# Three of seven pairs of chunk 0's gradient product moved into the opening part, and the steps that go with it

## The chip, the cores and the metric

The kernel runs on one core of a Trainium2 chip, as one launch. The metric is the device time of that launch in microseconds, lower is better. PE is the matrix engine (TensorE), ACT the scalar engine, DVE the vector engine, POOL the GpSimd engine; SP only issues DMAs. PE writes its products to PSUM banks, and ACT or DVE must copy ("evict") them to SBUF before a bank is used again.

## What is computed

A four-layer network and its gradients, with S = 2048 positions, D = 448 features, F = 1792 hidden features, in bfloat16. Cut to what matters:

```python
def A(q, k, v, shift_k, ssm_k, ssm_D):     # long convolution, done by FFT
    kv = short_conv(k, shift_k) * v
    y = irfft(rfft(kv, 2S) * rfft(ssm_k, 2S))[:S] + kv * ssm_D
    return q * y
def B(x, w1, w2):
    return silu(x @ w1) @ w2
x = A_q
x = x + A(layernorm(x), ...)
x = x + B(layernorm(x), w1, w2)
x = x + A(layernorm(x), ...)               # the same k, v: y is the same
x = x + B(layernorm(x), w1, w2)
# outputs: x, and the gradients of q, k, v, shift_k, ssm_k, ssm_D, w1, w2 for a given grad_out
```

## The kernel before

**Opening part** (`_ssm_prefix`). It computes y once. The spectrum of ssm_k is made first (A1K, Z, Ka in the lines); then kv goes through a two-stage FFT. Stage 1 ends at A1kv, which is turned by PE transposes in seven groups (`turn`, L367; a `ps_tr` tile and a copy each). Then a loop over 14 chunks of 1024 columns (`_fft_stage2` with `cons_prod`, L461) does, for each chunk: two matmuls into `ps_s`, an eviction, one DVE product `pab` with the spectrum and its half-swapped copy, and, two chunks later, 16 short matmuls into `ps_v` with an eviction. Evictions go to ACT or DVE by `_Bal.pick`, which adds up estimated loads. The half-swapped copy is made by 14 DMAs on POOL's queue (L440); after them come the stores of the spectrum (L445). All PSUM tiles here share four slots, tag "A". Last, eight `ps_y` tiles give Ysb, all evicted by ACT (L497). The layer norm of chunk 0's input (`ln0`, `_ln_steps`) is fed into this part by `next(ln0)`.

**Main part** (`Main.run`). Positions are worked in four chunks of 512. The blocks, named by the letters of the `weave` patterns, are:

- H: product with w1, seven pairs of hidden tiles; ACT computes silu (aT) and copies the raw value (dT), so a pair costs ACT two evictions. L is the layer, 0 or 1.
- O: product of aT with w2, added to X; eight half steps of 7 matmuls, two to each tile of 128 positions; its two PSUM banks are freed by the DVE addition L699.
- G: product of a gradient with w2 transposed, seven pairs, evicted by ACT to ghT, later multiplied by the slope of silu on DVE.
- N: product of ghT with w1 transposed, eight half steps, then the layer norm's gradient on DVE.
- T: PE transposes with an ACT copy to nT or gT, the input of H or G.

`_products` (L504) yields the seven pairs of H or G: pair 0 has 8 matmuls, pairs 1, 3, 5 have 10 (four of them on half the rows), pairs 2, 4, 6 have 6. PE's order is the program's order; the other engines are ordered by a scheduler from its own estimates. `slope` (L683) is the ACT pass that turns dT into slopes after each H block. `fwd0(c)` and `fwd0b(c)` compute, on DVE with a power on POOL, layer 0's normalised and gated input of chunk c and from it n01, which T transposes for the next H.

For chunk 0, grad_out is transposed at the end of the opening part into gT0, a piece of X (L484 to 488). Its G block runs as three pairs before the first H (L816) and four behind the first O (L828). Chunk 1's G follows: three pairs at L831, and four at c = 1 in the pattern `OGGOGGOTOT` (L858). The input of chunk 1's G is loaded by eight transposing DMAs on SP's queue (`load_gT`). Loads on SP in this part are, in order: x0c for chunk 1, w2sb, w1T, gb, then these.

Of the kernel before, what the change touches and what calls it, by code (L numbers as in the profile page):

```python
# [10 lines left out]
FP32 = mybir.dt.float32  # L11
# [249 lines left out]
def _ln_steps(k, pool, c, src, si, n_g, groups=((0, 4),), pin=False, eng=None, behind=None, store=()):  # L261
    nc = k.nc
    for lo, hi in groups:
        n = hi - lo
        st = pool.tile([P, 4, 6], FP32, name="ln_st", tag="ln_st", bufs=1)
        mv = pool.tile([P, 4, 2], FP32, name="ln_mv", tag="ln_mv", bufs=2)
        for tl in range(lo, hi):
            with ExitStack() as es:
                if behind:
                    es.enter_context(k.tc.issue_after(behind[tl].ins))  # L270
                i = nc.vector.bn_stats(out=st[:, tl, :], in_=src(tl))
            if pin:
# [6 lines left out]
        k.ln_pow = nc.gpsimd.tensor_tensor(out=r[:, lo:hi], in0=ve[:, 0:n], in1=k.mhalf[:, 0:n], op=ALU.pow)  # L279
        if eng is nc.scalar:  # L280
            nmr = pool.tile([P, 4], FP32, name="ln_nmr", tag="ln_nmr", bufs=1)
            nc.vector.scalar_tensor_tensor(out=nmr[:, lo:hi], in0=mv[:, lo:hi, 0], scalar=-1.0, in1=r[:, lo:hi], op0=ALU.mult, op1=ALU.mult)
        for tl in range(lo, hi):
            if eng is nc.scalar:
                nc.scalar.activation(n_g[:, tl, :], src(tl), ACT.Identity, bias=nmr[:, tl:tl + 1], scale=r[:, tl:tl + 1])
            else:
                k.ln_last = nc.vector.tensor_scalar(out=n_g[:, tl, :], in0=src(tl), scalar1=mv[:, tl, 0:1], scalar2=r[:, tl:tl + 1], op0=ALU.subtract, op1=ALU.mult)  # L287
# [10 lines left out]
def _ssm_prefix(k):  # L298
# [4 lines left out]
    with ExitStack() as es:  # L303
# [60 lines left out]
        bal.reset()  # L364
        A1Kf = A1K[:].rearrange("p a c n s -> p (a c n s)").rearrange("p (a b) -> p a b", b=P)

        def turn(src, dst, g):  # L367
            pt = psum.tile([P, 16, P], BF16, name="ps_tr", **a_)
            for i in range(16):
                nc.tensor.transpose(pt[:, i, :], src[:, 16 * g + i, :], k.ident[:])  # L370
            _copy(nc, bal.pick(2048, dve_ns=0.53), dst[:, 16 * g:16 * g + 16, :], pt[:])

        for jq in range(4):
            pt = psum.tile([DC, ND, 4, P], BF16, name="ps_kT", **a_)
# [50 lines left out]
        for h in range(2):  # L425
            for i, jq in enumerate((1, 2, 3, 0)):
                kvt = conv(h, jq)
                if prev:
                    stage1_kv(*prev)
                prev = (h, jq, kvt)  # L430
                if h == 0:
                    for g in (2 * i, 2 * i + 1):
                        if g < 7:
                            turn(A1Kf, Z, g)
                else:
                    _fft_stage2(k, Z, psum, cons_ka, range((0, 4, 8, 11)[i], (4, 8, 11, 14)[i]))
                    next(ln0, None)
        for _ in ln0:
            pass
        for i in range(7):  # L440
            _swap_halves_dma(k, KB, Ka, 2048 * i, 2048 * (i + 1), nc.gpsimd)
        stage1_kv(*prev)
# [4 lines left out]
        nc.sync.dma_start(out=k.w1sb[:, 0:3, :], in_=k.B_w1[0:384].rearrange("(c p) f -> p c f", p=P))  # L447
        nc.sync.dma_start(out=k.w1sb[64:128, 3, :], in_=k.B_w1[384:448, :])
        nc.sync.dma_start(out=k.w1sb[0:64, 3, 2 * P:], in_=k.B_w1[320:384, 2 * P:])
        nc.gpsimd.memset(k.w1sb[0:64, 3, 0:2 * P], 0.0)  # L450


# [2 lines left out]

        A1f = A1kv[:].rearrange("p a c n s -> p a (c n s)")
        for g in range(7):
            turn(A1f, Zkv, g)
        hold = []

        def cons_prod(ci, ps):  # L461
            sl = slice(ci * 1024, (ci + 1) * 1024)
            xs = Zf[:, sl]
            _copy(nc, bal.pick(1024), xs, ps[:])
            if ci % 2 == 1:
                st = nc.gpsimd.dma_start(out=k.SPEC_d["KV"][:, (ci - 1) * 1024:(ci + 1) * 1024], in_=Zf[:, (ci - 1) * 1024:(ci + 1) * 1024])
            if ci == 3:
                with tc.issue_after(st.ins):
                    nc.gpsimd.memset(k.w2T[0:64, 3, 0:2 * P], 0.0)
            pab = work.tile([P, 2, 1024], BF16, name="pab", tag="pab", bufs=3)  # L470
            nc.vector.tensor_tensor(out=pab[:], in0=xs.rearrange("p (a c) -> p a c", a=1).to_broadcast([P, 2, 1024]), in1=ZK[:, :, sl], op=ALU.mult)
# [8 lines left out]
        k.X = k.wk.tile([P, NT, D], BF16, name="X", tag="WX")  # L480
        k.gT0 = k.X[:].rearrange("p t d -> p (t d)")[:, 11 * D:11 * D + 2048].rearrange("p (b t) -> p b t", b=ND)
        for pa, pb, cj in hold:
            _fft_inv_stage2_chunk(k, pa, pb, False, B1, cj, psum, halves=cj == NCI - 1)
        pt = psum.tile([P, ND, 512], BF16, name="ps_t", tag="A", bufs=4)  # L484
        for b, (lo, hi) in enumerate(BLK):
            for tl in range(4):
                nc.tensor.transpose(pt[:, b, tl * P:(tl + 1) * P], k.gb0[:, tl, lo:hi], k.ident[:])
        nc.vector.tensor_copy(k.gT0, pt[:])

        B1v = B1.rearrange("p a (c n s) -> p a c n s", c=2, n=16)  # L490
        for i in range(8):
            py = psum.tile([P, 2, 512], FP32, name="ps_y", tag="A", bufs=4)
# [45 lines left out]
class Main:  # L538
# [165 lines left out]
    def G(self, gT, res, dT=None, dv=()):  # L704
        nc, k = self.nc, self.k
        half = lambda h: self.t([P, NF // 2, 512], f"ghT{h}", "T", 5)
        res[:] = [half(0)]
        gh = res
        for fp, ps in _products(nc, lambda: self.banks("ps_g"), self.w2T, gT):
# [74 lines left out]
    def run(self, es):  # L784
# [34 lines left out]
        aT, dT1 = r  # L819
# [17 lines left out]
        for c in range(4):  # L837
# [38 lines left out]
            if c < 3:  # L876
                r = []
                if c == 0:
                    weave("NTNTNHNNHHNNHHNHH", N=n, T=self.T(self.n0[1][1], nT), H=self.H(c + 1, 0, nT, r, (10, 11)))
# [23 lines left out]
            if c < 3:  # L903
                r = []
                nT = self.nT()
                weave("NNTNTNHNNHHNNHHHH", N=n, T=self.T(self.n1[1], nT), H=self.H(c + 1, 1, nT, r, (10, 11)))
            else:
                weave("NJNNJNNJNNJN", N=n, J=jg)
        jobs.pool = None
# [473 lines left out]
```

## Time and profile before

| what | value |
|---|---|
| time before, median of 3 runs | 716.89 us (713.9 to 718.23) |
| the profiled execution's own time | 716.31 us |
| its span in the trace | 714.5 us |
| PE busy | 689.3 us, 96% of the span |
| DVE busy / ACT busy | 486.2 us / 444.2 us |
| POOL busy | 123.3 us |

The sum of a prediction is made against the profiled execution: 716.31 us, of which 714.5 us is the span and 1.8 us lies around it. In a timeline, the first two columns are start and duration in us; the bracket at the end is the time the engine sat idle before that row, and what ended that idle time. Neighbouring instructions of one kind are merged into a row with a count, and a row's duration ends with its last instruction, so that back to back rows overlap a little.

### The profile page before, as it was taken

How to read it: one execution, taken by the hardware profiler on the slowest of the kernel's cores; microseconds unless marked ns; L12 is line 12 of the kernel's file. 1: busy time of each engine (PE TensorE's matmuls, PEld its weight loads, DVE VectorE, ACT ScalarE, POOL GpSimd, SP SyncE). 2: the span in 40 equal slices, each digit the busy share in tenths (PEclk: the TensorE clock that was granted, in tenths of full speed). 3: DMA queues.
4: the chain of work that ended last, by engine and by line, in shares of the span. 5: the costliest groups of instructions: out<-in, count | busy, mean ns of one | idle time of the engine just before them, and what ended most of it. 6: DMA issues, size and time to landing. Idle time of an engine off the chain costs nothing.

```text
span 714.5 us, 12786 instructions
## 1 busy us (share of the span) xinstructions
PE 689.3 (96%) x5008; PEld 380.9 (53%) x5008; DVE 486.2 (68%) x1106; ACT 444.2 (62%) x582; POOL 123.3 (17%) x208
## 2 busy tenths in 40 slices
PE   6997899999999999999999999999999999999998
PEld 4886654434444444444444444544566666656655
DVE  4788776758887747877279723934258769869790
ACT  3878877686777868778677685132755555545200
POOL 1034420111011100111001100001212223353130
PEclk9999899999999999999999999999999999999999
DMA  9949998659969999499975999089999897879962
GB/s 303 305 146 234 342 287 255 168 139 270 236 146 235 215 240 242 116 243 231 224 179 133 233 229 365 3 187 249 309 413 357 291 343 245 266 274 377 354 181 95
DMA packets 196237, 172.59 MB, mean 242 GB/s; under 512 B 143090, under 2 KB 174194, under 8 KB 195024
## 3 DMA queue, kind: packets, MB, share of 16 engines
q1 hardware_dynamic: 181280, 115.30, 61.3%
q0 software_dynamic: 13344, 52.54, 20.9%
q10 hardware_dynamic: 1552, 3.94, 1.5%
q8 instruction: 39, 0.64, 0.4%
q14 instruction: 22, 0.18, 0.1%
HBM read 73.25 MB, written 60.10 MB: 187 GB/s over the span
## 4 chain that ended last, share of the span: by engine, by line
PE 62%; issue 8%; DVE 5%; ACT 4%; DMA 3%; POOL 2%; POOLq 0%; DVEq 0%; ACTq 0%
PE ps_d L995 12%; PE ps_n L741 12%; PE ps_h L513 11%; PE ps_g L513 10%; PE ps_o L695 7%; PE ps_d L1030 3%; ACT dT L688 2%; DMA ksf<-KS_d 1%; PE ps_t L580 1%; PE ps_gK L1305 1%; PE ps_tr L1211 1%; POOL rstd L279 1%; PE ps_d L1065 1%; PE ps_s L206 1%; DVE n L287 1%
## 5 line engine op out<-in xcount | busy, mean ns | idle before, releaser
L995 PEld LDWEIGHTS <-dstat 128*128 128x128 bf16 x768 | 72.5, 98 | 61.1
L513 PE MATMUL ps_h<-nT,w1sb 128*128 128x512 bf16 (+1 forms) x448 | 97.4, 380 | 2.6 <-ACT dT L678 1.9
L741 PE MATMUL ps_n<-w1T,ghT 128*128 128x448 bf16 x448 | 92.5, 353 | 0.8 <-DVE ghT L866 0.8
L695 PE MATMUL ps_o<-w2sb,aT 128*128 128x448 bf16 x448 | 88.5, 352 | 0.0
L513 PE MATMUL ps_g<-nT,w2T 128*128 128x512 bf16 (+1 forms) x392 | 82.9, 380 | 0.1
L723 ACT CAST ghT<-ps_g 128x512 bf16<-128x512 f32 (+1 forms) x74 | 54.1, 760 | 41.5 <-PE ps_g L513 41.2
L673 ACT ACTIVATE aT<-ps_h 128x512 bf16<-128x512 f32 (+1 forms) x82 | 60.0, 759 | 29.2 <-PE ps_h L513 27.6
L513 PEld LDWEIGHTS <-w1sb 128*128 128x128 bf16 (+1 forms) x448 | 35.5, 97 | 59.7 <-issue 25.4
L741 PEld LDWEIGHTS <-ghT 128*128 128x128 bf16 x448 | 43.2, 98 | 42.3 <-DVE ghT L866 1.7
L695 PEld LDWEIGHTS <-aT 128*128 128x128 bf16 x448 | 43.5, 98 | 40.1
L513 PEld LDWEIGHTS <-w2T 128*128 128x128 bf16 (+1 forms) x448 | 35.4, 97 | 55.1 <-issue 20.8
L915 DVE SCALAR_TENSOR_TENSOR lb_v<-lb_u,n 128x448 bf16<-128x448 bf16 x48 | 30.0, 624 | 46.8 <-ACT lb_u L745 46.3
L279 POOL TENSOR_TENSOR rstd<-ln_ve,mhalf 128x2 f32<-128x2 f32 (+2 forms) x27 | 23.0, 851 | 198.8 <-DVE ln_ve L277 198.8
L688 ACT ACTIVATE dT<-dT 128x1024 bf16<-128x1024 bf16 (+1 forms) x64 | 55.0, 940 | 0.1
L995 PE MATMUL ps_d<-n1m,dstat 128*128 128x448 bf16 x224 | 48.6, 352 | 0.0
L995 PE MATMUL ps_d<-n3m,dstat 128*128 128x448 bf16 x224 | 48.6, 352 | 0.0
L678 ACT CAST dT<-ps_h 128x1024 bf16<-128x1024 f32 (+1 forms) x50 | 42.8, 872 | 0.0
L745 ACT ACTIVATE lb_u<-ps_n,rstd 128x448 bf16<-128x448 f32 x32 | 20.7, 647 | 34.5 <-PE ps_n L741 26.3
L995 PE MATMUL ps_d<-X,dstat 128*128 128x448 bf16 x160 | 34.2, 353 | 0.0
L995 PE MATMUL ps_d<-go,dstat 128*128 128x448 bf16 x160 | 33.7, 353 | 0.0
L581 ACT COPY nT<-ps_t 128x1024 bf16<-128x1024 bf16 x20 | 20.2, 1008 | 18.7 <-PE ps_t L580 18.7
L866 DVE TENSOR_TENSOR ghT<-dT,ghT 128x512 bf16<-128x512 bf16 (+2 forms) x24 | 18.1, 778 | 19.2 <-ACT ghT L723 17.0
(217 smaller groups left out, 1245.1 us busy)
## 6 DMA issues: line engine op xcount, KB each, us to landing
dstat<-g_d SPq DMA_DIRECT2D x28, 512.0 KB, 5.6
dstat<-a_d SPq DMA_DIRECT2D x23, 512.0 KB, 7.1
a_d<-turned SPq DMA_DIRECT2D x16, 512.0 KB, 4.1
g_d<-turned SPq DMA_DIRECT2D x16, 512.0 KB, 3.9
a_d<-turned SPq DMA_DIRECT2D x16, 384.0 KB, 3.3
g_d<-turned SPq DMA_DIRECT2D x16, 384.0 KB, 3.3
N_d<-n POOLq DMA_DIRECT2D x10, 448.0 KB, 4.6
spec_K<-ZK POOLq DMA_DIRECT2D x7, 512.0 KB, 7.7
```

Of the source, the lines that this page charges most:

```text
L279: k.ln_pow = nc.gpsimd.tensor_tensor(out=r[:, lo:hi], in0=ve[:, 0:n], in1=k.mhalf[:, 0:n], op=ALU.pow)
L513: nc.tensor.matmul(ps(u, u + 1)[:, 0, :], lhsT=wT[h, b, ft * P:(ft + 1) * P], rhs=rhs[h, b, :], start=start, stop=stop)
L673: self.last_silu = nc.scalar.activation(aT[hh][:, o:o + hi - lo, :], ps(lo, hi), ACT.Silu)
L678: nc.scalar.copy(self.dpart(dT, 2 * fp + lo, 2 * fp + hi), ps(lo, hi))
L688: self.nc.scalar.activation(d[:, o:o + n, :], d[:, o:o + n, :], ACT.Derivative_silu)
L695: nc.tensor.matmul(po[:, :D], lhsT=aT[ft // 7][:, ft % 7, tl * P:(tl + 1) * P], rhs=self.w2sb[:, ft, :], start=(ft == 0), stop=(ft == NF - 1))
L723: nc.scalar.copy(g, ps(lo, hi))
L741: nc.tensor.matmul(pn[:, :D], lhsT=gh[ft // 7][:, ft % 7, tl * P:(tl + 1) * P], rhs=self.w1T[:, ft, :], start=(ft == 0), stop=(ft == NF - 1))
L745: nc.scalar.activation(u0[:], pn[:, :D], ACT.Identity, scale=k.rstd[2 * L + 1][:, t:t + 1], accum_out=cp[:, tl, 0:1])
L915: nc.vector.scalar_tensor_tensor(out=v[:], in0=u0, scalar=-1.0 / D, in1=n_t, op0=ALU.mult, op1=ALU.mult, accum_out=cp[:, 1:2])
L995: self.nc.tensor.matmul(ps[:, :D], lhsT=st[:, t, :], rhs=mov[:, t, :], start=(first and t == 0), stop=(last and t == NT - 1))
L1030: nc.tensor.matmul(ps[ft][:, :D], lhsT=get(t), rhs=mov[:, t, :], start=ft not in seen, stop=(last[ft] == i and t == hi - 1))
```

## The change

Chunk 0's gradient is transposed in front of the 14-chunk loop instead of behind it. Three blocks of its product with w2 (pairs 0, 1 and 2) are issued in the opening part: behind chunk 6, behind chunk 10 and behind the loop. The other four pairs run in front of the first H. The first seven hidden tiles (gh0) live in X, in rows that chunk 2 and 3 fill later; so the G of chunk 0's layer 0 uses that place too. Chunk 1's whole G block follows the first O, and nothing of G is left at c = 1. With it go: the layer norm `ln0` starts earlier (its steps also run in the loop's first half), w1sb is loaded through POOL's queue behind the spectrum stores, a memset of w2T comes earlier, the seven turns are dealt out to ACT and DVE by hand, `fwd0b(1)` follows the six slope products, and two weave patterns are changed (the first of N of layer 1 with H of chunk 1, the second of N of layer 0 with H of layer 1). Of the three loads of w1sb the diff shows one.

```diff
 def _ln_steps(...)
         k.ln_pow = nc.gpsimd.tensor_tensor(out=r[:, lo:hi], ..., op=ALU.pow)
+        yield
 def _ssm_prefix(k):
-        def turn(src, dst, g):
+        def turn(src, dst, g, eng=None):
...
-            _copy(nc, bal.pick(2048, dve_ns=0.53), dst[:, 16 * g:16 * g + 16, :], pt[:])
+            _copy(nc, eng or bal.pick(2048, dve_ns=0.53), dst[:, 16 * g:16 * g + 16, :], pt[:])
...
                             turn(A1Kf, Z, g)
+                    next(ln0)
                 else:
                     _fft_stage2(k, Z, psum, cons_ka, ...)
                     next(ln0, None)
-        for _ in ln0:
-            pass
+        nc.gpsimd.memset(k.w2T[0:64, 3, 0:2 * P], 0.0)
         for i in range(7):
             _swap_halves_dma(k, KB, Ka, 2048 * i, 2048 * (i + 1), nc.gpsimd)
...
-        nc.sync.dma_start(out=k.w1sb[:, 0:3, :], ...)
+        nc.gpsimd.dma_start(out=k.w1sb[:, 0:3, :], ...)
...
         for g in range(7):
-            turn(A1f, Zkv, g)
+            turn(A1f, Zkv, g, nc.vector if g % 3 else nc.scalar)
+        bal.reset()
         hold = []
+        k.X = k.wk.tile([P, NT, D], BF16, name="X", tag="WX")
+        Xf = k.X[:].rearrange("p t d -> p (t d)")
+        k.gh0 = Xf[:, 8 * D:].rearrange("p (a s) -> p a s", s=512)
+        pt = psum.tile([P, ND, 512], BF16, name="ps_t", tag="A", bufs=4)
+        for b, (lo, hi) in enumerate(BLK):
+            for tl in range(4):
+                nc.tensor.transpose(pt[:, b, tl * P:(tl + 1) * P], k.gb0[:, tl, lo:hi], k.ident[:])
+        g3 = k.gb0[:]....[:, 0:1536]
+        g1 = Xf[:, 4 * D:4 * D + 512]...
+        nc.vector.tensor_copy(g3, pt[:, 0:3])
+        nc.vector.tensor_copy(g1, pt[:, 3:4])
+        bal.add("dve", 1.3)
...
+        k.g20 = _products(nc, lambda: k.banks(), k.w2T, Sets())
+        def g_step():
+            fp, ps = next(k.g20)
+            _copy(nc, bal.pick(1024), k.gh0[:, 2 * fp:2 * fp + 2, :], ps(0, 2))
 
         def cons_prod(ci, ps):
...
+            if ci in (6, 10):
+                g_step()
         _fft_stage2(k, Zkv, psum, cons_prod)
-        k.gT0 = ...
+        g_step()
         for pa, pb, cj in hold:
             _fft_inv_stage2_chunk(k, pa, pb, False, B1, cj, psum, halves=cj == NCI - 1)
-        pt = psum.tile([P, ND, 512], BF16, name="ps_t", tag="A", bufs=4)
-        for b, (lo, hi) in enumerate(BLK):
-            for tl in range(4):
-                nc.tensor.transpose(pt[:, b, tl * P:(tl + 1) * P], k.gb0[:, tl, lo:hi], k.ident[:])
-        nc.vector.tensor_copy(k.gT0, pt[:])
 Main.run:
-        g20 = self.G(k.gT0, gh2, dv=(2,))
+        g20 = self.G(None, gh2, dv=(5,), first=k.gh0)
-        steps("GGtttG", G=g20, t=self.T2(self.n0[0][1], nT))
+        steps("GGtttGG", G=g20, t=self.T2(self.n0[0][1], nT))
...
-        steps("GGGG", G=g20)
         next(g20, None)
+        steps("GGGG", G=g21)
         nT = self.nT()
         steps("tGtGtGt", G=g21, t=self.T2(self.n1[1], nT))
...
             if c == 0:
                 weave("O" * 4, O=o)
-                self.fwd0b(1)
...
             for lo, hi in ((0, 4), (4, 7), (7, 8), (8, 12), (12, 13), (13, 14)):
                 nc.vector.tensor_tensor(out=g, in0=self.dpart(dT2, lo, hi), in1=g, op=ALU.mult)
+            if c == 0:
+                self.fwd0b(1)
...
                 if c == 0:
-                    weave("NTNTNHNNHHNNHHNHH", ...)
+                    weave("NNTNTNHNNHHNNHHHH", ...)
...
-                g = self.G(gT, gh1, dT0)
+                g = self.G(gT, gh1, dT0, first=None if c else k.gh0)
...
             if c < 3:
-                weave("NNTNTNHNNHHNNHHHH", ...)
+                weave("NNTNTNHNHNHHNHHNH", ...)
```

More of the change, by code (lines that the diff above doesn't have):

```diff
@@ L446, in _ssm_prefix @@
         k.w1sb = k.wk.tile([P, ND, F], BF16, name="w1sb", tag="WB")
-        nc.sync.dma_start(out=k.w1sb[:, 0:3, :], in_=k.B_w1[0:384].rearrange("(c p) f -> p c f", p=P))
-        nc.sync.dma_start(out=k.w1sb[64:128, 3, :], in_=k.B_w1[384:448, :])
-        nc.sync.dma_start(out=k.w1sb[0:64, 3, 2 * P:], in_=k.B_w1[320:384, 2 * P:])
+        nc.gpsimd.dma_start(out=k.w1sb[:, 0:3, :], in_=k.B_w1[0:384].rearrange("(c p) f -> p c f", p=P))
+        nc.gpsimd.dma_start(out=k.w1sb[64:128, 3, :], in_=k.B_w1[384:448, :])
+        nc.gpsimd.dma_start(out=k.w1sb[0:64, 3, 2 * P:], in_=k.B_w1[320:384, 2 * P:])
         nc.gpsimd.memset(k.w1sb[0:64, 3, 0:2 * P], 0.0)
@@ L457, in _ssm_prefix, with __getitem__, banks @@
         for g in range(7):
-            turn(A1f, Zkv, g)
+            turn(A1f, Zkv, g, nc.vector if g % 3 else nc.scalar)
+        bal.reset()
         hold = []
+        k.X = k.wk.tile([P, NT, D], BF16, name="X", tag="WX")
[5 more added lines that the diff above has]
+                nc.tensor.transpose(pt[:, b, tl * P:(tl + 1) * P], k.gb0[:, tl, lo:hi], k.ident[:])
+        g3 = k.gb0[:].rearrange("p t d -> p (t d)")[:, 0:1536].rearrange("p (b s) -> p b s", s=512)
+        g1 = Xf[:, 4 * D:4 * D + 512].rearrange("p (b s) -> p b s", s=512)
+        nc.vector.tensor_copy(g3, pt[:, 0:3])
+        nc.vector.tensor_copy(g1, pt[:, 3:4])
+        bal.add("dve", 1.3)
+        class Sets:
+            def __getitem__(self, at):
+                h, b, cols = at
+                return g3[h, b, cols] if b < 3 else g1[h, 0, cols]
+        def banks():
+            ps = psum.tile([P, 2, 512], FP32, name="ps_g", tag="A", bufs=4)
+            return lambda lo, hi: ps[:, lo:hi, :]
+        k.banks = banks
+        k.g20 = _products(nc, lambda: k.banks(), k.w2T, Sets())
+        def g_step():
+            fp, ps = next(k.g20)
+            _copy(nc, bal.pick(1024), k.gh0[:, 2 * fp:2 * fp + 2, :], ps(0, 2))
         def cons_prod(ci, ps):
@@ L465, in cons_prod @@
             if ci % 2 == 1:
[L466 to L469, printed above, removed]
+                nc.gpsimd.dma_start(out=k.SPEC_d["KV"][:, (ci - 1) * 1024:(ci + 1) * 1024], in_=Zf[:, (ci - 1) * 1024:(ci + 1) * 1024])
             pab = work.tile([P, 2, 1024], BF16, name="pab", tag="pab", bufs=3)
@@ L476, in cons_prod @@
                 _fft_inv_stage2_chunk(k, pa, pb, False, B1, cj, psum)
+            if ci in (6, 10):
+                g_step()
         _fft_stage2(k, Zkv, psum, cons_prod)
-        k.X = k.wk.tile([P, NT, D], BF16, name="X", tag="WX")
-        k.gT0 = k.X[:].rearrange("p t d -> p (t d)")[:, 11 * D:11 * D + 2048].rearrange("p (b t) -> p b t", b=ND)
+        g_step()
         for pa, pb, cj in hold:
             _fft_inv_stage2_chunk(k, pa, pb, False, B1, cj, psum, halves=cj == NCI - 1)
-        pt = psum.tile([P, ND, 512], BF16, name="ps_t", tag="A", bufs=4)
-        for b, (lo, hi) in enumerate(BLK):
-            for tl in range(4):
-                nc.tensor.transpose(pt[:, b, tl * P:(tl + 1) * P], k.gb0[:, tl, lo:hi], k.ident[:])
-        nc.vector.tensor_copy(k.gT0, pt[:])
         B1v = B1.rearrange("p a (c n s) -> p a c n s", c=2, n=16)
@@ L702, in O, with G @@
             yield
-    def G(self, gT, res, dT=None, dv=()):
+    def G(self, gT, res, dT=None, dv=(), first=None):
         nc, k = self.nc, self.k
         half = lambda h: self.t([P, NF // 2, 512], f"ghT{h}", "T", 5)
-        res[:] = [half(0)]
+        res[:] = [half(0) if first is None else first]
+        if gT is None:
+            k.banks = lambda: self.banks("ps_g")
+            prods = k.g20
+        else:
+            prods = _products(nc, lambda: self.banks("ps_g"), self.w2T, gT)
         gh = res
-        for fp, ps in _products(nc, lambda: self.banks("ps_g"), self.w2T, gT):
+        for fp, ps in prods:
             if fp == 3:
@@ L878, in run @@
                 if c == 0:
-                    weave("NTNTNHNNHHNNHHNHH", N=n, T=self.T(self.n0[1][1], nT), H=self.H(c + 1, 0, nT, r, (10, 11)))
+                    weave("NNTNTNHNNHHNNHHHH", N=n, T=self.T(self.n0[1][1], nT), H=self.H(c + 1, 0, nT, r, (10, 11)))
                 else:
@@ L905, in run @@
                 nT = self.nT()
-                weave("NNTNTNHNNHHNNHHHH", N=n, T=self.T(self.n1[1], nT), H=self.H(c + 1, 1, nT, r, (10, 11)))
+                weave("NNTNTNHNHNHHNHHNH", N=n, T=self.T(self.n1[1], nT), H=self.H(c + 1, 1, nT, r, (10, 11)))
             else:
```

## The prediction

> **What bounds the kernel now.** I read the page's busy times first, then the busy times by stretch, then each engine's timeline where PE has holes. PE is busy 689.3 of 714.5 us, so 25 us are to be had, and the stretches show that most of them lie in the opening part:
>
> ```profile
> 54.00:72.00 18.00, 14.28 (x190) 12.03 (x189) 14.86 (x19) 14.61 (x16) 7.79 (x14) 0.92 0.95 233
> 72.00:90.00 18.00, 15.23 (x176) 11.47 (x174) 14.82 (x13) 15.15 (x16) 7.05 (x14) 0.89 1.03 349
> 140.00:160.00 20.00, 18.02 (x91) 7.12 (x90) 11.13 (x28) 16.05 (x30) 2.41 (x4) 1.00 0.45 117
> 250.00:300.00 50.00, 49.94 (x278) 23.55 (x277) 34.61 (x97) 38.04 (x52) 3.02 (x4) 1.00 0.87 205
> ```
>
> After length come PE, PEld, DVE, ACT, POOL, clock, DMA. From 54 to 90 PE lacks 6.5 us; from 250 to 300 nothing. Filling the first hole helps only if DVE and ACT there, 82% busy, let it. Their timelines in the chunk loop, DVE first, then ACT:
>
> ```profile
> 68.97 2.36 DVE L471 TENSOR_TENSOR pab<-A1K,ZK 128x2048 bf16<-128x2048 bf16 x2 [2.16 <-ACT A1K L111]
> 72.98 2.43 DVE L471 TENSOR_TENSOR pab<-A1K,ZK 128x2048 bf16<-128x2048 bf16 x2 [1.66 <-DMA ZK<-ZK]
> 77.12 1.23 DVE L112 CAST A1K<-ps_s 128x1024 bf16<-128x1024 f32 x1 [1.70 <-PE ps_s L217]
> ...
> 91.53 2.36 DVE L471 TENSOR_TENSOR pab<-A1K,ZK 128x2048 bf16<-128x2048 bf16 x2
> 95.05 0.69 DVE L112 CAST A1kv<-ps_v 128x512 bf16<-128x512 f32 x1 [1.16 <-PE ps_v L230]
> ```
>
> ```profile
> 65.32 2.72 ACT L285 ACTIVATE na<-x0c,ln_nmr,rstd 128x448 bf16<-128x448 bf16 x4
> 67.94 2.81 ACT L111 CAST A1K<-ps_s 128x1024 bf16<-128x1024 f32 x3
> ```
>
> DVE loses 3.4 us up to 77 and almost nothing from there to 93.9: DVE sets the loop's pace. The first `pab` waits for an eviction that stands behind the norm (na). PE meanwhile waits 3.65 us, and the clock drops to 0.50 from 69.0 to 75.8. The end of the H block at c = 1, PE:
>
> ```profile
> 233.27 3.40 PE L513 MATMUL ps_h<-nT,w1sb 128*128 128x512 bf16 x16
> 237.13 3.63 PE L513 MATMUL ps_h<-nT,w1sb 128*128 128x512 bf16 x16 [0.47 <-ACT dT L678]
> 240.60 6.78 PE L695 MATMUL ps_o<-w2sb,aT 128*128 128x448 bf16 x35
> 247.22 3.40 PE L513 MATMUL ps_g<-nT,w2T 128*128 128x512 bf16 x16
> ...
> 252.00 3.39 PE L513 MATMUL ps_g<-nT,w2T 128*128 128x512 bf16 x16
> ...
> 256.56 0.61 PE L580 MATMUL ps_t<-ident,n 128*128 128x128 bf16 x8
> ...
> 258.77 1.49 PE L741 MATMUL ps_n<-w1T,ghT 128*128 128x448 bf16 x7
> ```
>
> The 32 matmuls of G are taken out of this stretch; they cover DVE's chain to n01, which T at 256.56 reads:
>
> ```profile
> 234.28 0.63 DVE L915 SCALAR_TENSOR_TENSOR lb_v<-lb_u,n 128x448 bf16<-128x448 bf16 x1 [3.09 <-ACT lb_u L745]
> ...
> 245.81 1.32 DVE L287 TENSOR_SCALAR n<-X,ln_mv,rstd 128x448 bf16<-128x448 bf16 x4 [1.15 <-POOL rstd L279]
> ```
>
> **The change part by part.** G of one chunk is 56 matmuls in 11.43 us; the moved pairs are 24 of them, 4.9 us less PE work in the main part. The rest is where that time comes back.
>
> *Opening part.* Added to the loop: 24 matmuls (4.9 us) and three evictions of 1024 (DVE 1.22, ACT 1.01 us). By the built order DVE takes two and ACT one; DVE gives one `ps_s` cast to ACT and takes one `ps_v`. DVE gains two casts, at a spacing of 1.13 us 2.3 us. Against it: DVE's losses of 1.66 and 1.70 us may go. The swap DMAs no longer share 57 to 67 us with w1sb, nor stand behind the power on POOL (3.25 us of waiting at 62.99), so the first should. The second came from the slow clock. The first `pab` comes little earlier: na is out of the way (2.6 us), but the third turn that ACT gets (1.87 us) and 0.6 us, by which na's four passes outlast ACT's 0.9 us holes in the loop's first half (0.65 us each, two to a turn), take most of it: about 68.6 instead of 68.97. I rolled the 14 chunks forward by hand from there with these spacings: last `pab` ends near 93.95 (93.89 before), `ps_y` starts near 95.8 (95.89). The transposes of gb0 (1.06 us) and their copies (about 1.3 us) fill the hole before the first `pab`; at the end they cost nothing before, as `ps_y` waited for the cast at 95.05 anyway. Sum -0.1. Bounds: -2 (all 3.4 us of loss and 0.4 gained, against 2.3, some more idle on ACT), +3.4 (PE stays at half clock for the same 6.8 us and nothing takes it up). I take -0.1, nearest to the rolled rows.
>
> *w1sb through POOL* starts near 77 instead of 57.7, 12 us at most to landing: before 90, needed at 109. Free. On POOL it stands ahead of the KV stores, whose landing ACT's first write to the new ghT waits for near 104; the last landed before 97 and the added 1.8 MB are 4.4 us at 400 GB/s: free by 3 us, else one for one. The memset of w2T (0.33 us) and the store of na move ahead of the swaps on POOL, which is 17% busy; the power of na (1.04 us) lets DVE wait once near 43, where it had 0.86 us of idle time. Free but for what the 0.6 us above holds.
>
> *In front of the first H.* Four pairs instead of three, the last two (16 matmuls, 3.3 us) behind T. Before: T ends 107.2, 6 matmuls, H at 109.2 after 0.55 us of waiting for nT. Now G's first 16 end at 106.0, T at 106.9, H starts 110.2: +1.0.
>
> *Behind the first O* PE still has 56 matmuls and three T; the third T waits for DVE as now (1.48 us). 0.
>
> *c = 0, N.* The slope products no longer wait behind n01, so the 0.77 us (`ghT`) goes, but n01 comes about 2 us later, near 172.3, and T now stands two half steps into N, at 171.5. Counted over the same work the stall falls from 1.5 to 0.9 us: -0.6.
>
> *gh0 in X.* Chunk 2's gate overwrites it at c = 1, near E+4.5 (below); its last reader on PE is done three H pairs before E, its transposing stores were issued by 217.8. Free.
>
> *Patterns.* A tail HHHH costs 0.47 us of waiting and 0.23 us inside (3.63 against 3.40), as ACT needs two evictions of 1.0 us to PE's 1.62 us. It leaves three places (-0.7 each) and enters one (+0.7).
>
> *c = 1 without G.* Let E be the end of H (240.6). Before, N starts at E+18.2. By PE alone it could start at E+11.8 (eight half steps of 1.32 and two T). But the new pattern puts the last N half step 1.6 us before E, not 7.2, so DVE's chain starts near E-0.5, not E-6.3. Before it took 12.85 us from there to n01. In the built order one cast (1.12) leaves it, a second and third X addition (1.1) and two slope products (1.13, 0.87, in place of most of POOL's 1.15) enter: about 14.0. So n01 is ready at E+13.5; T, which PE reaches at E+9.3, waits 4.3 us, and N starts at 13.6 + 0.45 + 1.32 + 0.45 = E+15.8. -2.4, and -0.7 by the pattern. Queued behind DVE's chain is also the addition that frees the first O bank, at E+6.2 instead of E+3.9: O's third tile waits 1 us from E+5.3. At c = 1 that is inside the same stall; at c = 2 it is +1.0 with -0.7: +0.3. At c = 3 there is no such chain: -0.7.
>
> Sum: -0.1 +1.0 -0.6 +0.7 -3.1 +0.3 -0.7 = -2.5; 716.3 - 2.5 = **713.8 us**. The profiled run is 0.6 below the median of the three.
>
> **The rivals.** (1) *The saving arrives*: DVE reaches n01 in time at c = 1. For it: DVE sat idle 3.09 us before 234.28. Against: the built order has the norm of the next chunk behind the last N chain. Gain 4.3 more: 709.5, about 1% faster.
> (2) *The loop turns slower*: a PE hole of about 2 us remains before the first `ps_v`, and a clock drop with more PE work behind it has no cover: +3.4 in place of -0.1, 717.3, slower than before. For: the drop at 69.0 came though the 3.4 us before it held 1 us of matmuls. Against: holes of 1.5 us (143.7) left the clock at 1.00. It decides if the clock falls again.
> [...]
> (3) *Chunk 1's gradient comes late*: G now reads its transposes right behind O, near 131 instead of 138.3. The last is issued at 121.7 and landing takes 2.4 to 8.6 us, so 130.3 at worst; the queue loses x0c and a store in between. If w2sb waits for the end of `ps_y`, it moves back some 6 us. At most 6.9 us would be lost: 720.7, slower. It decides past 131.
>
> **How the numbers follow.** Forecast 0.56, rival 1 0.18, rival 2 0.14, rival 3 0.06, others with more than 1% lost 0.06. A difference under 1% (7 us) is about what a measurement of this kernel can't tell from none. Faster by more: two thirds of rival 1, 0.12, and 0.02 of the forecast with a good loop: 0.14. Slower by more: 0.06. Same: 0.80. The range takes in rival 2 and most of rival 1 and leaves out 0.18 (a third of rival 1, rival 3, the last): 708.8 to 718.5; the forecast's own is 711.5 to 716.
>
> **What would show it.** `ps_y` starts between 94 and 99 us, with DVE nearly without holes in the loop; the first H about 6.8 us after Ysb's last copy (109.22 - 103.41 = 5.8 before); a T at c = 1 idle some 4 us before it on DVE's n; no 0.47 us wait in the tails of layer 0's H. Wrong if that T does not wait, if the clock is at 0.5 in the loop, or if G near 131 waits for a DMA.

## The result

| kernel | time, median | times shown | ratio to before, 95% interval |
|---|---|---|---|
| before | 715.86 us | 713.9 to 718.23 | |
| after | 723.02 us | 719.52 to 727.3 | 1.0105 [1.0058, 1.0151] |

The change costs 1%, clear of the noise by the interval. The profiled execution of after took 723.42 us, its span is 721.6 us, 7.1 us more than before's. PE's busy time grows by 1.7 of them (691.0 against 689.3 us); the other 5.4 us are waits. These are PE's longest waits by sum from 100 to 470 us, the first of before, then the first three of after; columns: who waited on whom, total us, times, longest.

```profile
PE ps_h L513 <- ACT dT L678: 1.9, 4, 0.5
```

```profile
PE ps_t L603 <- DVE n L288: 4.8, 2, 2.7
PE ps_h L536 <- ACT dT L701: 3.3, 8, 0.5
PE ps_o L718 <- DVE X L722: 2.1, 2, 1.0
```

The first row of after is new: T waits twice for n01, 4.8 us. The second is the old wait for dT, eight times instead of four. The third is the third tile of O, at c = 1 and c = 2. The stretches that the prediction showed read like this after:

```profile
54.00:72.00 18.00, 16.14 (x193) 12.82 (x192) 14.48 (x14) 14.86 (x14) 11.41 (x21) 0.91 0.98 255
72.00:90.00 18.00, 16.32 (x185) 11.18 (x183) 14.58 (x14) 15.03 (x17) 3.61 (x8) 1.00 0.90 347
...
250.00:300.00 50.00, 46.22 (x248) 22.29 (x248) 37.55 (x107) 35.49 (x47) 4.75 (x6) 0.97 0.86 215
```

In the opening part PE's idle time falls from 6.5 to 3.5 us (also 3.5 us from 50.73 to 86.73, which is the same work, as `ps_cv` starts 3.3 us sooner in this execution of after). From 250 to 300, where PE had none, it now has 3.8 us, and a clock of 0.97. PE's timeline at c = 1, with E, the end of H, at 244.35:

```profile
241.40 0.39 PE L536 MATMUL ps_h<-nT,w1sb 64*128 64x512 bf16 x2 [0.40 <-ACT dT L701]
...
250.85 4.13 PE L718 MATMUL ps_o<-w2sb,aT 128*128 128x448 bf16 x21 [1.04 <-DVE X L722]
257.68 1.37 PE L603 MATMUL ps_t<-ident,n 128*128 128x128 bf16 x8 [2.70 <-DVE n L288]
258.89 2.37 PE L718 MATMUL ps_o<-w2sb,aT 128*128 128x448 bf16 x7
...
261.90 1.92 PE L770 MATMUL ps_n<-w1T,ghT 128*128 128x448 bf16 x7
```

G is gone, and T waits where G was. The half step of O behind it takes 2.37 us where seven such matmuls take 1.49: the clock is at one half. N starts at E+17.55, before at E+18.2. DVE in the same stretch:

```profile
242.31 1.23 DVE L699 CAST dT<-ps_h 128x1024 bf16<-128x1024 f32 x1 [5.53 <-ACT aT L696]
244.06 0.62 DVE L945 SCALAR_TENSOR_TENSOR lb_v<-lb_u,n 128x448 bf16<-128x448 bf16 x1 [0.53 <-ACT lb_u L774]
...
250.18 1.15 DVE L722 TENSOR_TENSOR X<-X,ps_o 128x448 bf16<-128x448 bf16 x2
...
257.23 1.31 DVE L288 TENSOR_SCALAR n<-X,ln_mv,rstd 128x448 bf16<-128x448 bf16 x4 [0.93 <-POOL rstd L279]
```

The chain that leads to n01 starts at 244.06, E-0.3 (before: 234.28, E-6.3). In front of it stands a cast, and ahead of that DVE is idle for 5.53 us. The addition that frees O's bank stands inside this chain.

To see where the time goes I divide the traces at the same work, from PE's first matmul into `ps_cv` to its last. "After, again" is the profile of a second run of after (below), in which the trace shows no fall of the clock. A stretch runs from block start to block start; O of chunk c, layer L, is written O(c,L).

| stretch, us | before | after | after, again | predicted change | change, again to before |
|---|---|---|---|---|---|
| first `ps_cv` to first `ps_y` | 69.70 | 72.32 | 70.68 | -0.1 | +0.98 |
| to the first H | 13.33 | 13.51 | 13.50 | +1.0 | +0.17 |
| to O(0,1) | 48.99 | 48.97 | 48.97 | 0 | 0 |
| to O(1,0): N at c = 0 | 35.01 | 38.97 | 37.34 | -0.6 and +0.7 | +2.33 |
| to O(1,1): first pattern of layer 0 | 47.38 | 47.66 | 47.66 | -0.7 | +0.28 |
| to O(2,0): c = 1 | 40.20 | 40.00 | 38.34 | -2.4 | -1.86 |
| to O(2,1): second pattern | 47.03 | 47.32 | 47.31 | -0.7 | +0.28 |
| to O(3,0): c = 2 | 45.48 | 46.60 | 46.61 | +1.0 | +1.13 |
| to O(3,1): third pattern | 47.02 | 47.33 | 47.30 | -0.7 | +0.28 |
| to PE's end | 291.25 | 292.90 | 291.45 | 0 | +0.20 |
| sum | 685.39 | 695.58 | 689.16 | -2.5 | +3.8 |

The first row compares a stretch at full clock with one that isn't: before's profile has the clock at half for 6.83 us in it (69.02 to 75.85). The part ahead of `ps_cv`, which the change doesn't touch, took 26.19 us before and 22.92 after: in that one execution the first `ps_s` started at 11.86 instead of 13.40 us, and from there to `ps_cv` it took 11.06 instead of 12.79. Without this the profiled loss would have been 10 us. In three stretches (opening part, c = 0, c = 1) after is 1.64, 1.63 and 1.66 us behind its own second run: in each the clock fell for 3.41 us.

### The profile page after: what moved, and what is told of

The parts are those of the page before. It is cut to its first block, busy times and chain, and to the rows that moved or that the text cites. A ratio compares the mean times of both kernels' runs of the same rounds, so it can differ in the third digit from the quotient of the medians.

```text
span 721.6 us, 12800 instructions
## 1 busy us (share of the span) xinstructions
PE 691.0 (96%) x5008; PEld 381.2 (53%) x5008; DVE 487.7 (68%) x1108; ACT 443.7 (61%) x580; POOL 124.8 (17%) x211
## 4 chain that ended last, share of the span: by engine, by line
PE 61%; issue 10%; DMA 9%; DVE 9%; ACT 6%; POOL 4%; SPq 0%; POOLq 0%; DVEq 0%; ACTq 0%
PE ps_n L770 11%; PE ps_g L536 11%; PE ps_d L1025 10%; PE ps_h L536 9%; PE ps_o L718 6%; PE ps_d L1060 3%; DMA dstat<-a_d 2%; DMA ZK<-ZK 2%; DMA out_dram<-q_g 1%; PE ps_t L603 1%; ACT A1K L111 1%; DVE n L288 1%; POOL rstd L279 1%; ACT aT L696 1%; DMA spec_K<-ZK 1%
## 5 line engine op out<-in xcount | busy, mean ns | idle before, releaser
L770 PE MATMUL ps_n<-w1T,ghT 128*128 128x448 bf16 x392 | 82.2, 354 | 0.0
L752 ACT CAST ghT<-ps_g 128x512 bf16<-128x512 f32 (+1 forms) x65 | 47.2, 752 | 37.9 <-PE ps_g L536 33.9
L770 PEld LDWEIGHTS <-ghT 128*128 128x128 bf16 x392 | 37.4, 98 | 36.8 <-issue 2.8
L699 DVE CAST dT<-ps_h 128x512 bf16<-128x512 f32 (+1 forms) x26 | 19.1, 768 | 28.2 <-ACT aT L696 28.1
```

The costliest lines, as they stand in the source:

```text
L770: nc.tensor.matmul(pn[:, :D], lhsT=gh[ft // 7][:, ft % 7, tl * P:(tl + 1) * P], rhs=self.w1T[:, ft, :], start=(ft == 0), stop=(ft == NF - 1))
```

## The experiments

Two theories stood. Theory 1: the order of the work on DVE makes n01 late at c = 0 and c = 1, and PE's wait then also lets the clock fall. Theory 2: G was needed as cover in these places, whatever DVE does. Beside them, for the prediction's own terms: the patterns, the opening part.

**Both edits at c = 0 undone** (e1_c0_old).

```diff
             if c == 0:
                 weave("O" * 4, O=o)
+                self.fwd0b(1)
...
-            if c == 0:
-                self.fwd0b(1)
...
-                    weave("NNTNTNHNNHHNNHHHH", ...)
+                    weave("NTNTNHNNHHNNHHNHH", ...)
```

> The changed kernel with the two edits at c = 0 undone: n01 of chunk 1 is again written ahead of the slope products, and N of layer 1 takes its old pattern NTNTNHNNHHNNHHNHH. Theory 1 (the order on DVE): in the changed kernel T at 173.2 waits 2.06 us for n01 because the slope products stand in front, the clock falls behind that wait, and the next O block starts 4.0 us later against the H block before it. Undone, T waits at most 1.5 us, the clock stays at 1.00 there, O starts near 193 instead of 196.7, and the time is about 3.5 us under the changed kernel's: near 719.5. Theory 2 (the loss at c = 0 belongs to G being gone from there or to the first hidden tiles lying in X): T still waits about 2 us, O stays within 1 us of 196.7, 722 to 724.

Measured: 721.76 us, 1.0058 [1.0037, 1.008]. T doesn't wait, the stretch to O(1,0) is 35.02 us (before 35.01), with the clock at 1.00. G and the first hidden tiles are placed as in after, so theory 2 falls for c = 0, by the wait and the stretch. The time doesn't decide it: it is 2.3 us above the 719.5 that theory 1 gave and close to theory 2's 722. At c = 1 the wait of 2.70 us and the fall of the clock are still there.

**Layer 0's pattern put back** (e2_l0_old).

```diff
-                weave("NNTNTNHNHNHHNHHNH", N=n, T=self.T(self.n1[1], nT), ...)
+                weave("NNTNTNHNNHHNNHHHH", N=n, T=self.T(self.n1[1], nT), ...)
```

> The changed kernel with only the pattern of N of layer 0 put back to NNTNTNHNNHHNNHHHH (three places). Theory 1 (the order on DVE, which the pattern sets): the last N half step lies 7 us before the end E of the H block again, DVE has n01 ready before PE reaches T at E+9.3, and N at c = 1 starts at about E+12 instead of E+17.55 (-5.5); the waits of 1.04 and 1.2 us of O's third tile at c = 1 and 2 go (the first lies in the same stall, so -1.2), the tails of H are 0.28 us cheaper three times (-0.8). Sum -7.5: near 715.5. Theory 2 (G's 32 matmuls are missing as cover, whatever the pattern): T at c = 1 still waits 2.5 us or more, N not before E+15, sum -4: 719.

Measured: 718.12 us, 1.001 [0.9988, 1.0033]. N at c = 1 starts at E+11.80, T waits for nothing, O(1,1) to O(2,0) takes 33.82 us, and the third tile of O waits nowhere. Theory 1 holds to 0.2 us in these stretches. The time is 2.6 us above the expected. Why is not shown for the median; in the profiled execution (720.57 us) the end was 6 us longer (275.2 us from the first N of chunk 3, 269.2 before). The clock fell in it once, at 595, and DVE waited 8.3 us for a load of `q_y`, where it waited 4.3 before.

**Both put back** (e3_both_old: the edits of e1 and e2).

> The changed kernel with both undone: the edits at c = 0 and the pattern of layer 0. What is left of the change is the opening part and the moved products. Theory 1: the two gains add, -3.5 and -7.5 from 723: 712, under the kernel before by about 4 us. Theory 2: 718 to 720, not under the kernel before.

Measured: 713.58 us, 0.9939 [0.9916, 0.9962]: under the kernel before, and 1.6 us above the expected 712. The clock was at 1.000 in all six executions. PE at c = 1, E at 243.40:

```profile
243.40 9.73 PE L718 MATMUL ps_o<-w2sb,aT 128*128 128x448 bf16 x49
252.97 0.61 PE L603 MATMUL ps_t<-ident,n 128*128 128x128 bf16 x8
253.41 1.49 PE L718 MATMUL ps_o<-w2sb,aT 128*128 128x448 bf16 x7
254.75 0.61 PE L603 MATMUL ps_t<-ident,n 128*128 128x128 bf16 x8
255.19 1.49 PE L770 MATMUL ps_n<-w1T,ghT 128*128 128x448 bf16 x7
```

There is no bracket in it: N follows at E+11.79 without a hole. All 6.4 us of the 32 matmuls are saved here (33.81 against 40.20 us).

**The kernel before with the new pattern of layer 0 alone** (e7_before_l0new: the edit of e2 the other way round, on the kernel before).

> The kernel before with nothing but the new pattern of layer 0, NNTNTNHNHNHHNHHNH in three places. G's 32 matmuls are still at c = 1. Theory 1: the tails of H each cost 0.3 us more (two waits of 0.40 us on dT instead of one of 0.47 and 0.23 inside), O's third tile waits about 1 us at c = 1 and 1.2 at c = 2, and T at c = 1, reached near E+16, waits little, as n01 comes near E+14: in all +2.5 to +3.5, 719. My prediction said the pattern is 0.7 us cheaper at each place: by that, 716 or less. Theory 2 (DVE's late chain costs as much with G there): T waits 2 us or more, 721.

Measured: 719.94 us, 1.0042 [1.0023, 1.0061]. Each place costs +0.30 or +0.31 us, and O's third tile waits at c = 1 and 2. PE at c = 1, E at 241.94:

```profile
248.44 1.49 PE L695 MATMUL ps_o<-w2sb,aT 128*128 128x448 bf16 x7 [1.04 <-DVE X L699]
...
258.88 0.61 PE L580 MATMUL ps_t<-ident,n 128*128 128x128 bf16 x8
```

With G in place T comes at E+16.9 and doesn't wait. So G is a cover for DVE's late chain, and only for the late one: taking it out gains 6.4 us with the old pattern and 2.8 us (41.18 to 38.34) with the new one.

**The kernel after once more** (after_again, no edit).

> The changed kernel itself once more, for how much of its loss comes and goes from one execution to the next. In the trace at hand PE waits 2.06 us at 173.2 and 2.70 us at 257.7 for n01, and the clock falls to 0.50 for 3.41 us behind each; its four executions had granted clocks of 0.993, 1.000, 0.995 and 0.995, and 719.5 us with 1.000. Theory 1 (the waits cost their length, the clock drop some 1.6 us each on top, in most executions): median 722 to 724, executions with clock 1.000 near 719.5, and the waits of 2.06 and 2.70 us are there in any case. Theory 2 (the first profile was an unlucky one): median 719 to 720, waits shorter.

Measured: 724.53 us, 1.0103 [1.0067, 1.0139]. The two waits are there (2.05 and 2.71 us) with the clock at 1.00. Taken together, the ten executions of after order by the granted clock: 719.5 and 719.8 us at 1.000, 721.3 at 0.997, 722.6 to 727.3 at 0.995, 723.4 to 729.3 at 0.993. The kernel before, measured beside it, has 716.0 to 719.1 us at 1.000 (median 716.6) and 717.4 over all 30. So about 3 us of the loss are there at full clock, and some 4 come in most executions together with a lower clock (three falls, as in after's first profile, are 4.9 us). Before loses less by it, 0.8 us in the median; in its profile the clock falls at the head of the chunk loop.

**Which of the two edits at c = 0** (both with layer 0's pattern old; the lines are those of e1). First n01 ahead of the slope products, with the new pattern (e4_n01_first).

> Layer 0's pattern old; at c = 0 n01 is written ahead of the slope products again, but N keeps the new pattern NNTNTNHNNHHNNHHHH. Theory 1 (it is the order on DVE that makes T late, not the pattern): T does not wait for n01 any more, N's second half step waits for ghT about 1.2 us instead of 0.78 (the T that stood in between has moved), and from O of chunk 0 to O of chunk 1 it takes 35.6 us (35.02 with both old, 37.4 with both new and no clock drop): 714 to 715. Theory 2 (the pattern): 37 us or more, 716 or more.

Measured: 714.96 us, 0.9977 [0.996, 0.9993]. T doesn't wait; N waits 0.57 and 0.77 us for ghT, and the tail 0.47 for dT; it takes 36.48 us to O(1,0), 0.9 more than theory 1 gave and 0.5 less than theory 2. Then the slope products ahead, with the old pattern (e5_c0pat_old).

> Layer 0's pattern old; at c = 0 the slope products stand ahead of n01 as in the changed kernel, but N has its old pattern NTNTNHNNHHNNHHNHH, so PE reaches T one half step (1.32 us) sooner. Theory 1 (the order on DVE): T waits about 3.4 us, and the stretch from O to O is 38.0 us without a clock drop and 39.6 with one: 717 to 720. Theory 2 (the pattern): T waits no longer than in the kernel before (1.5 us), 35 to 36 us, 714.

Measured: 720.57 us, 1.0041 [1.0021, 1.006]. T waits 3.38 us, as theory 1 had it, and behind it the clock was at half: the next two half steps of N take 2.82 and 2.28 us, where one takes 1.49 at full clock, and the granted clock of this execution is 0.995. It is 40.51 us to O(1,0), where 39.6 were expected with a fall. So the place of n01 on DVE decides whether T waits; the pattern alone costs 1.5 us as well (36.48 against 35.02), through the waits for ghT and dT.

**A third half step of N ahead of T** (e6_third_N, with layer 0's pattern old).

```diff
-                    weave("NNTNTNHNNHHNNHHHH", N=n, T=self.T(self.n0[1][1], nT), ...)
+                    weave("NNNTNTHNNHHNNHHHH", N=n, T=self.T(self.n0[1][1], nT), ...)
```

> Layer 0's pattern old; at c = 0 as in the changed kernel but for the pattern, NNNTNTHNNHHNNHHHH: a third half step of N covers 1.32 us of T's wait of 2.06. Nothing is taken away or added. Theory 1 (a hole of 2 us lets the clock fall in some executions, one of 0.7 does not): T waits 0.75 us, the stretch from O to O is 36.05 us instead of 37.4 (without drop) or 39.0 (with one), the granted clock is 1.000 in nearly all executions, where the same kernel with the 2.06 us wait had 1.000 in 2 of 12: median 715, 3 us under it. Theory 2 (the clock has nothing to do with that hole): only the 1.32 us are won, the clock stays mixed, 717.

Measured: 716.32 us, 0.999 [0.9974, 1.0006]. T waits 0.74 us, as expected, but H now waits 0.84 us for nT, so the stretch is 37.03 us, only 0.34 less than with the longer wait (37.37 in e2). The clock was 1.000 in 7 of 12 executions and never under 0.997, with the 2.06 us wait in 2 of 12 and 0.995 in six. The time is 1.8 us under that of e2 (718.12), where 3 were expected. That the hole pulls the clock down fits this, and the windows in the next section show it; that its cover gains its length was wrong, as the copy of nT took the next place on the path.

**Filled holes** (e10_fill_tr, e11_fill_mm). Useless work is put ahead of T, so that PE isn't idle in the two holes; first transposes, then matmuls:

```diff
+        for i in range(fill):
+            nc.tensor.transpose(pt[:, i % 2, 0:P], k.ident[:], k.ident[:])
```

```diff
+        if fill:
+            pf = k.psum.tile([P, 512], FP32, name="ps_f", tag="tr", bufs=1)
+            for i in range(fill):
+                nc.tensor.matmul(pf[:, :D], lhsT=k.ident[:], rhs=self.w2sb[:, 0, :], start=True, stop=True)
```

> The changed kernel with work of no use in its two holes: 32 transposes of the identity ahead of T at c = 0 (1.8 us, its wait is 2.06) and 44 ahead of T at c = 1 (2.45 us of 2.70). Nothing is moved and nobody waits longer. Theory 1 (an idle PE lets the clock fall, whatever its work is): no more drops near 174 and 258, so 719.7 in nearly all executions instead of 724, clock 0.998 to 1.000 (the opening part may still drop once). Theory 2 (transposes don't keep the clock up): as the changed kernel, 723 to 724.5, clock 0.993 to 0.997. Theory 3 (the drops don't hang on the holes): the same as theory 2, and e11 as well.

> The same with ordinary matmuls of no use in the holes, 9 of 0.19 us ahead of T at c = 0 and 13 ahead of T at c = 1. Theory 1 and 2: no more drops near 174 and 258, 719.7 in nearly all executions, clock 0.998 to 1.000. Theory 3: 723 to 724.5, clock 0.993 to 0.997.

Measured: 721.68 us, 1.0062 [1.0039, 1.0085], with transposes, and 725.1 us, 1.0104 [1.007, 1.0139], with matmuls. PE at c = 0 with transposes:

```profile
174.35 1.95 PE L601 MATMUL ps_t<-ident 128*128 128x128 bf16 x32
176.58 1.37 PE L605 MATMUL ps_t<-ident,n 128*128 128x128 bf16 x8 [0.28 <-DVE n L288]
```

In both profiles the clock stays at 1.00 in both places, and the stretches are those of after's second run (37.35 and 38.33 us with transposes, 37.34 and 38.33 with matmuls; 37.34 and 38.34 there). With transposes the clock was 1.000 in five of seven executions and never under 0.997. With matmuls it was 1.000 in three of six, and the time doesn't follow: one of these took 726.4 us, and in the profiled one (0.995) the clock fell in the opening part and at 521, and the first N of chunk 3 to the end took 273.7 us (after's second run 269.4). So theory 1 holds for the two holes, by the traces and the executions with transposes. Both medians are misses, 2.0 and 5.4 us above the expected 719.7; with transposes a fall in the opening part had been allowed for, and with matmuls nothing shows why.

**w1sb back on SP's queue** (e8_w1_sp, on top of e3; the three loads as before).

> Both parts of the order put back as in e3_both_old, and also the three loads of w1sb back on SP's queue (issued near 57, beside the swap DMAs). Theory 1 (my prediction: the swaps share the DMA engines with w1sb, so DVE's product waits 1.7 us for the swapped spectrum): that wait comes back near 72, PE idles again at the head of the chunk loop, in some executions with the clock at 0.50, and from PE's first ps_cv to the first H it takes 85 to 86 us instead of 84.2: 715. Theory 2 (the swaps are early enough anyway, as they no longer stand behind the power on POOL): 84.2 us, 713.6.

Measured: 711.4 us, 0.9928 [0.99, 0.9955]. DVE's waits at the head of the loop are 1.13 and 1.26 us, on ACT and PE, as in after's first profile (1.12 and 1.27), and none is on the swapped spectrum. The 85.81 us to the first H are what theory 1 gave, but by a fall of the clock at 70.4: after's first profile, with w1sb on POOL and a fall there, has 85.83. So theory 2: w1sb on SP costs nothing that shows, and this is the best of the versions, though its interval overlaps that of e3.

**The early transposes alone, on the kernel before** (e9_tr_early).

```diff
         hold = []
+        k.X = k.wk.tile([P, NT, D], BF16, name="X", tag="WX")
+        k.gT0 = ...
+        pt = psum.tile([P, ND, 512], BF16, name="ps_t", tag="A", bufs=4)
+        ...
+        nc.vector.tensor_copy(k.gT0, pt[:])
...
-        nc.vector.tensor_copy(k.gT0, pt[:])
```

> The kernel before, and of the change only this: chunk 0's grad_out is transposed and copied in front of the 14-chunk loop instead of behind it. Theory 1: the 16 transposes (0.9 us) and the copy fill part of the 3.65 us in which PE waits for the first product, but DVE, which sets the pace, gets a copy of 1.2 us there: from ps_cv to the first H 83 to 84 us as before (83.03), 716.5, and the clock still falls in the opening part in most executions. Theory 2 (the hole's filling is what the change's opening part lives on): no clock drop, 81 to 82 us, 715.

Measured: 715.29 us, 0.9997 [0.9975, 1.0019]. PE's wait falls from 3.65 to 2.75 us, `ps_cv` to the first H from 83.03 to 82.26 us, and the clock falls for some 3.4 us instead of 6.83 (PE's rows run at half speed from about 70.0 to 73.4); it was 1.000 in six of twelve executions. Between the two expectations, and no difference in the time that can be told.

## Why the prediction was wrong

The forecast was 713.8 us with a range to 718.5; the time is 723.02. A loss of over 1% had a chance of 0.06. Three steps failed. The chain to n01 at c = 0 was put 2.2 us too early, so T's stall grew where it was to shrink. The new pattern of layer 0 was priced by the waits that it removes, without those that it makes. And falls of the clock in the main part were put at nothing. At full clock the change costs 3.8 us where 2.5 were to be gained; of these 6.3 us, 2.9 lie in the three places of the pattern, 2.2 at c = 0, 1.1 in the chunk loop less 0.8 in front of H, and the other 0.9 at c = 1, c = 2 and the end. The falls come on top. By terms:

*Opening part and the first H.* Sum right, parts not: +0.9 was forecast, +1.15 came at full clock (against before with its fall), but as +0.98 in the loop (for -0.1) and +0.17 in front of H (for +1.0). The first product comes 43.36 us behind the first `ps_cv` (42.78 before), not sooner, as I had it. That DVE's 1.66 us wait for the swapped spectrum came from w1sb's traffic is not borne out by e8. The swaps take up to 13.5 us to land in before, where w1sb is issued beside them from 57.73 us, and at most 8.9 in after, where it comes behind them. But in e8 it is issued beside them again, and no product is listed as waiting for one. What held the swap up before is not shown. The clock did fall here in the profiled execution, which is rival 2's condition; its price was 1.64 us, not 3.5.

*c = 0, forecast +0.1 with the tail, came +2.33 and +3.96 with the clock.* This is the first step that failed. I had n01 complete near 172.3 and T waiting from 171.5. PE, DVE and POOL there:

```profile
173.19 1.63 PE L603 MATMUL ps_t<-ident,n 128*128 128x128 bf16 x8 [2.06 <-DVE n L288]
```

```profile
167.79 1.90 DVE L894 TENSOR_TENSOR ghT<-dT,ghT 128x2048 bf16<-128x2048 bf16 x3
...
170.20 0.61 DVE L722 TENSOR_TENSOR X<-X,ps_o 128x448 bf16<-128x448 bf16 x1
...
170.94 0.17 DVE L277 TENSOR_SCALAR ln_ve<-ln_mv 128x4 f32<-128x4 f32 x1
172.74 1.31 DVE L288 TENSOR_SCALAR n<-X,ln_mv,rstd 128x448 bf16<-128x448 bf16 x4 [1.63 <-POOL rstd L279]
```

```profile
171.10 0.54 POOL L724 DMA_DIRECT2D out_dram<-X  x1 [4.71 <-DVE ln_ve L277]
171.66 1.04 POOL L279 TENSOR_TENSOR rstd<-ln_ve,mhalf 128x4 f32<-128x4 f32 x1
```

The same two steps before:

```profile
169.16 1.32 DVE L287 TENSOR_SCALAR n<-X,ln_mv,rstd 128x448 bf16<-128x448 bf16 x4 [0.40 <-POOL rstd L279]
```

```profile
167.45 1.67 POOL L279 TENSOR_TENSOR rstd<-ln_ve,mhalf 128x4 f32<-128x4 f32 x1 [0.59 <-DVE ln_ve L277]
```

The products and an addition stand ahead of n01. Then POOL issues a store (0.54 us) and works on the power, and DVE is idle for 1.63 us where it was idle for 0.40 before. POOL isn't slower: from the end of `ln_ve` to the end of `rstd` it takes 1.59 us, before 1.75. But before, DVE had a product (0.96 us) and an addition (0.62) to do meanwhile, and now these are done. The four passes end at 174.05, 5.73 us behind N's start at 168.32. They ended 1.67 us behind it before (N at 168.81), and the forecast had 3.5: so they come 2.2 us later than forecast. The forecast's 2 us have room for the products alone (1.56 and 0.76 us), and none for the addition (0.6) and the part of the power that nothing covers now (1.2). T reads a pass at a time, so it is slowed beyond its wait: in after's second run, without the fall, 1.37 us for eight transposes that take 0.61. The wait of 2.06 and these 0.76 us stand where I had 0.9, so the stall grows by 1.3 from the 1.5 of before instead of falling by 0.6; the tail's +0.7 came (0.47 in front of HHHH's last pair, 0.23 in it), and 0.3 are left over.

*The patterns, forecast -0.7 each, came +0.28 each.* The direction was wrong. The new pattern has no tail HHHH, but it has two pairs HH with one half step of N between them, and each costs a wait of 0.40 us on dT. Counted from start to start, over what two H take without a wait (3.23 us), the two cost 1.14 us and the tail HHHH 0.87. I counted the wait that goes and no wait that comes. Alone, on the kernel before, the pattern costs the same (e7).

*c = 1, forecast -2.4, came -1.86 at full clock and -0.20 with the fall.* Mechanism and size of the wait were right: I had T waiting 4.3 us with 1.0 of it at O's third tile moved ahead, and there are 1.04 and 2.70 us, and 0.76 in T. In the second run N starts at E+16.3, forecast E+15.8. What I left out is the clock, 1.66 us.

*c = 2, forecast +1.0, came +1.13*: right. *Behind O(3,1), forecast 0*, came +0.20 and +1.65.

*The clock.* I had looked for a fall in the opening part alone and set it aside in the main part, as a hole of 1.5 us (143.7) left it at 1.00. These are the 3.41 us ahead of after's first fall, the first fall itself, and the 3.41 us ahead of the other two; then the same hole as that at 170.61 in e2, where the clock stayed, and a filled one in e10:

```profile
64.79:68.20 3.41, 1.63 (x16) 0.83 (x15) 2.78 (x4) 3.29 (x4) 1.86 (x4) 1.00 1.06 251
68.20:71.61 3.41, 3.41 (x27) 2.67 (x25) 2.29 (x3) 2.03 (x3) 1.72 (x4) 0.50 1.00 304
170.61:174.02 3.41, 1.19 (x6) 0.36 (x4) 1.74 (x8) 0.73 (x2) 1.58 (x2) 1.00 1.14 324
255.94:259.35 3.41, 1.44 (x11) 0.86 (x12) 2.48 (x7) 0.26 (x1) 1.76 (x2) 1.00 1.18 190
```

```profile
171.85:175.26 3.41, 1.79 (x10) 0.71 (x8) 1.74 (x8) 0.72 (x2) 1.58 (x2) 1.00 1.15 320
```

```profile
174.28:177.69 3.41, 2.90 (x41) 2.26 (x39) 1.74 (x7) 0.72 (x2) 1.58 (x2) 1.00 1.19 283
```

PE (the second number) is busy 1.2 to 1.6 of 3.41 us ahead of each fall. Half clock for 3.41 us on a busy PE is 1.7 us of lost work, and 1.64, 1.63 and 1.66 were measured. In after's second run the same holes stood (2.05 and 2.71 us), and the clock didn't fall. The traces of before and after hint at why. In after the falls start at 68.20, 174.02 and 259.35 us, 31 and 25 times 3.413 us apart; in before at 69.02 and, behind PE's last matmul, at 714.14, 189 times. Divide each of these two traces, from 35 us to PE's last matmul, into stretches of 3.413 us counted from its falls: PE is busy 29% of the one ahead of before's fall (from 65.61 us) and 48, 35 and 42% of those ahead of after's; of every other stretch at full clock it is busy 57% or more, and no fall follows. In e2 the hole of 2.06 us, from 173.64 to 175.70, is shared by two such stretches (171.85 lies 124 times 3.413 us ahead of e2's fall at 595.1); PE is busy 52% of the first, and the clock stays. The hole of 1.5 us leaves PE busy 57% (140.70 to 144.12 in before). So it seems to count how a hole lies to these stretches. That is my reading of these three traces; no run tests it by itself, and after's second run has no fall to count from.

The transposes of e10 did no less for the clock than the matmuls of e11: without the useless transposes PE would be busy 33% and 21% of the 3.41 us from 174.28 and from 256.20 in e10 (an estimate, leaving them out of the trace), with them it is 85% and 93%, and the clock stayed at 1.00 in both places, as in e11.

*Rival 1* was the mechanism of value: with layer 0's old pattern, all 6.4 us arrive at c = 1 (e2 and e3). It failed in after for the reason that the prediction gave against it, the norm of the next chunk behind the last N chain. *Rival 3* didn't come: G at 130.90 waits for no transfer.

Open: from the first N of chunk 3 to PE's end it took 268.9 to 275.2 us over the fourteen profiles, although nothing was edited there; DVE's waits for loads of `q_y` in it add up to 4.5 us in one (e8) and 12.8 us in another (after), but don't go along with it: e2, with the longest end, has 9.6 us of them. No experiment was made on it.

## What to carry to other kernels

Before work is taken from in front of an instruction that depends on another engine, put that engine's chain on the same time axis, and move it earlier first. An order that costs little while PE has other work to cover it (1.0 us at c = 1 in e7) costs much more once that work is gone (4.5 us there, 38.34 against 33.82), and here the change moved the chain later in the same step as it took the cover. Count for a new weave pattern the waits that it makes, not only those it removes.

## What the runs showed of the hardware

- A fall of the clock to one half lasts 3.41 us three times in after, and 6.83 in before and in e7. One of 3.41 us costs 1.63 to 1.66 us where PE is busy (after against its second run).
- In before and after, PE is busy 29 to 48% of the 3.41 us ahead of each fall that stands before its last matmul, and 57% or more of every other stretch of 3.413 us, counted from the falls, at full clock from 35 us to that matmul. A hole of 2.06 us left 35% of such a stretch in after, and a fall followed; in e2 it left 52%, and none did.
- The executions of after range from 719.5 to 729.3 us. Three falls make 4.9 us of that; the rest is not explained.
- With 32 and 44 transposes in the two holes (e10) the clock was at 1.00 there, from 171 to 180 and from 255 to 266 us, as with 9 and 13 matmuls (e11).
- The start of the program takes a different time in each execution: PE's first `ps_cv` starts at 22.92 us in after and at 27.25 in e4. PE's first row, which waits for a load, starts at 4.41 us in e11 and at 5.49 in e6, and behind it the matmuls run at different speeds: 28 into `ps_s` take 6.41 us in after and 8.14 in its second run. Two profiles are compared from `ps_cv` on, not from the start of the span.
